# A Fourier-mixing and MLP kernel: one fold of the input rows is taken back, and the first transfers are put in another order

## The chip, the cores and the metric

The kernel runs on one core of a Trainium2 chip. The metric is the device time of one execution in microseconds. Three runs of the kernel before took 1938.29, 1939.47 and 1940.64 us; the median is 1939.47 us. A program that starts once does everything; the tables of sines and cosines are inputs, made ahead.

The engines are named as the profile names them: PE is TensorE (matmuls), PEld its weight loads, DVE is VectorE, ACT ScalarE, POOL GpSimd, and SP issues most of the transfers (SPq is its DMA queue).

## The reference

```python
batch, seq, dim = (8, 3008, 256)           # x: float32
n_tokens, d_model, d_ff = (24064, 256, 2048)   # w_in, w_out

def _attn_ref(x):
    X = np.fft.fft(x, axis=1)
    X = np.fft.fft(X, axis=2)
    return X.real.astype(np.float32)

def _moe_ref(x, w_in, w_out):
    h = x @ w_in
    r = np.maximum(h, 0.0)
    g = r * r
    return (g @ w_out).astype(np.float32)
```

The result of the first is reshaped to 24064 x 256 and goes into the second. Written out, the first is a transform of 3008 rows and one of 256 columns, of which the real part is kept. The weights come as 64-bit floats, which the kernel takes apart as words and turns into float32.

## The kernel before

With S = 3008 rows, the sums over n are folded by the symmetries of sine and cosine. The host sorts the rows so that n, S - n, S/2 - n and S/2 + n stand together for n from 0 to S/4. Sums and differences of these four, and of column pairs, leave 753 values of n. They are put into seven tiles of up to 128 rows in four classes: class 0, n = 0 mod 4 of the first half (1 tile), class 1, n = 2 mod 4 of the first half (1 tile), class 2, the odd n of the first half (tiles 2 and 3, 96 and 92 rows), class 3, the second half (tiles 4, 5 and 6). A class is multiplied with its own piece of the tables `cosT` and `sinT`, which lie in on-chip memory for the whole run. (The words that come with the change name the fold by "rows n of 2 mod 4"; in this code it is the tiles of class 2, `TWO` and `TWO + 1`.)

Class 3 is folded once more in batches 1 to 7 (n with its mirror), and in the kernel before class 2 is too: the second tile is loaded in reversed order, turned against the first, and two half-sized products take the place of a full one.

```python
    TWO = ODD0 - 2                 # ODD0 = 4, the first tile of class 3
    HALF2 = S // 32                # 94 rows
    ...
    def load_x(b, t):
        ...
        if b and t == TWO + 1:
            xt[b, t] = xp.tile([P, 4, D], F32, name="xt", tag="x")
            for p in range(0, ROWS2, R):
                at = TILES[TWO][1] + step * (2 * HALF2 - p - R)
                nc.sync.dma_start(out=xt[b, t][p:p + R], in_=x[b, at:at + step * (R - 1) + 1:step])
            return
    ...
    # in fold(b, t): the sums of the four rows (f_s, f_d, f_sc, f_dc, f_w), and for a folded tile
        def f_turn():
            w = w_of(t)
            if i != 1:
                st["v"], st["w"] = w_of(t - 1), w
                nc.vector.stream_shuffle(w[r], w[r], REVERSE)
            ...
            nc.scalar.copy(st["f0"][rows], st["v"][rows, 0])

        def f_even():
            v, w, a = st["v"][rows, 0], st["w"][rows, 0], st["f0"][rows]
            tt(out=v, in0=a, in1=w, op=ALU.add)
            tt(out=w, in0=a, in1=w, op=ALU.subtract)
        # f_sine: four products on ScalarE; f_odd: two scalar_tensor_tensor on VectorE
```

The products on TensorE, once for each batch, `which` (cosine or sine of the rows) and `kp` (even or odd k):

```python
            EVEN = ((0, 0, n2), (1, n2, n2), (2, 2 * n2, n1))     # n2 = 95 or 94, n1 = 189 or 188

            def even_n():
                st["ps"] = psd.tile([P, 512], F32, name="pd", tag="d")[0:n]
                for c, at, nk in EVEN:
                    if b and c == 2:
                        st["half"] = once_more(st["ps"][:, at:], c, nk)
                    else:
                        product(st["ps"][:, at:at + nk], c)       # L501: each tile of the class, nk columns
                copy_4()

            def once_more(ps, c, nk):                             # the products of L578
                nq = (nk + 2) // 2 if kp else (nk + 1) // 2
                pairs, rows = ((((TWO, TWO + 1),), HALF2), (((ODD0, ODD0 + 1), (ODD0 + 2, NT)), P))[c == 3]
                for part in range(2):
                    ...
                    for i, pair in enumerate(pairs):
                        nc.tensor.matmul(to, folded[b, pair[part != which]][0:rows, kp, PART[which]][:, 0:n],
                                         columns(tab, pairs[0][i] if c == 3 else TWO, o)[0:rows],
                                         start=i == 0, stop=i == len(pairs) - 1)
                if not kp:
                    return ps[:, 0:nk]
                a = hp.tile(...)                                  # for odd k: a copy on ScalarE,
                nc.scalar.copy(a, ps[:, 0:nq])                    # and join_odd: two operations on VectorE
                return a, ps[:, nq:2 * nq]
```

The steps that follow multiply with w_in (L664, L665, by way of the columns' transform G1 and G2), square on ScalarE, and multiply with w_out (L717, or L704 in the first steps). The folds and products of batch b + 1 are done in pieces between the steps of batch b, on VectorE, ScalarE and TensorE.

The first phase loads the first batch, both tables and the first weights on one queue, in this order, while VectorE folds:

```python
    for t in range(2):
        load_x(0, t)
    ...
    begin_win(0)                               # words of pair 0 of w_in: load, then convert
    ...
    load_table(cosT, cos_s, (2, 3))
    load_x(0, 6)
    load_table(cosT, cos_s, range(ODD0, NT))   # 3 transfers of 377 columns
    load_table(sinT, sin_s, range(ODD0, NT))   # 3 transfers of 377 columns
    win[1] = load(pair_in(1))                  # the second pair of w_in, 2 transfers
    load_table(sinT, sin_s, range(ODD0))       # 10 small transfers, of 95 or 189 columns
    win[2] = load(pair_in(2))                  # the third pair
    ...
    q_part("odd0", "odd1", "odd2")             # sine products on TensorE, tiles 4, 5, 6
    copy_e = win[0][2]()
    begin_win(1)                               # VectorE: L262, L267 and later L272 to L275
    for_q(3)
    q_part("even0", "even1", "even2")          # sine products, tiles 0 to 3
    awake(12)                                  # matmuls without use, to keep TensorE busy
    rounded(1)
    begin_win(2)                               # L262, L267 for the third pair
    for kp in range(2):
        for nm in ("join_4", "join_2", "lo"):
            groups[1, kp, nm]()                # VectorE: L538, L540
    spread_e()                                 # TensorE: L642, needs Qt
```

Each transfer of the queue waits, by a semaphore that the tile framework gives it in turn, until the transfer eight before it has landed.

Of the kernel before, what the change touches and what calls it, by code (L numbers as in the profile page):

```python
# [8 lines left out]
F32 = mybir.dt.float32  # L9
# [4 lines left out]
P = 128  # L14
R = 32
# [67 lines left out]
def kernel(  # L83
# [12 lines left out]
    nc = tc.nc  # L96
    B, NROW, _, D = x.shape
    S = out.shape[0] // B
# [35 lines left out]
    xt = {}  # L134
# [3 lines left out]
    ODD0 = NT - 3  # L138
# [4 lines left out]
           [(0, P, H // 2)] + [(H // 2 + p, 2 * HALF - P - p - R, R) for p in range(0, H // 2, R)]]  # L143
    assert H == P and REST <= H // 2 and TILES[ODD0][0] == 3 and TILES[ODD0 + 1][1] == TILES[ODD0][1] + P

    TWO = ODD0 - 2
    HALF2 = S // 32
    ROWS2 = TILES[TWO][3]
    assert TILES[TWO][0] == TILES[TWO + 1][0] == 2 and HALF2 <= ROWS2 < HALF2 + R and ROWS2 % R == 0

    def load_x(b, t):
        c, r0, step, rows = TILES[t]
        if b and c == 3:
            xt[b, t] = xp.tile([P, 4, D], F32, name="xt", tag="x")
            for p, first, count in ODD[t - ODD0]:
                nc.sync.dma_start(out=xt[b, t][p:p + count], in_=x[b, S // 8 + 1 + first:S // 8 + 1 + first + count])
            return
        if b and t == TWO + 1:
            xt[b, t] = xp.tile([P, 4, D], F32, name="xt", tag="x")
            for p in range(0, ROWS2, R):  # L160
                at = TILES[TWO][1] + step * (2 * HALF2 - p - R)
                nc.sync.dma_start(out=xt[b, t][p:p + R], in_=x[b, at:at + step * (R - 1) + 1:step])
            return

        while rows % 15 and rows % 16 and r0 + step * rows < NROW:
            rows += 1

        pool, tag = (gp, "g") if b == 0 and t < NT - NX else (xp, "x")
        xt[b, t] = pool.tile([P, 4, D], F32, name="xt", tag=tag)
        nc.sync.dma_start(out=xt[b, t][0:rows], in_=x[b, r0:r0 + step * (rows - 1) + 1:step])  # L170
# [151 lines left out]
    PQE = {}  # L322
    PART = (slice(0, H + 1), slice(H + 1, D))
    REVERSE = list(range(R - 1, -1, -1))

    turn = const.tile([P, 3, 3], F32, name="turn")

    def make_turn():
        for i, t in enumerate((ODD0, ODD0 + 1, TWO)):
            for a, tab in enumerate((cosT, sinT, sinT)):  # L330
                r = slice(0, TILES[t][3])
                nc.scalar.mul(turn[r, a, i:i + 1], tab[r, 1, PLACE[t]:PLACE[t] + 1], -1.0 if a == 2 else 1.0)
# [5 lines left out]
    def part_table(tab, t):  # L338


        nk, at = NC[0][TILES[t][0]], PLACE[t]
        rows = TILES[t][3]
        v = tab[0:rows, 0, at:at + nk]
        a = op.tile([P, nk], F32, name="tp", tag="os")[0:rows]
        nc.scalar.mul(a, v, rows_used if t == ODD0 + 1 else 1.0)
        nc.scalar.copy(v[:, 0:(nk + 1) // 2], a[:, 0::2])
        nc.scalar.copy(v[:, (nk + 1) // 2:], a[:, 1::2])

    def columns(tab, t, part):

        nk, at = NC[0][TILES[t][0]], PLACE[t]
        nq = (nk + 1) // 2
        return tab[:, 0, at + part * nq:at + (nk if part else nq)]

# [21 lines left out]
    def fold(b, t):  # L376


        odd, two = b > 0 and t >= ODD0, b > 0 and t == TWO + 1
        r = slice(0, P if odd else ROWS2 if two else TILES[t][3])  # L380
        st = {}

        def new(pool, nm, shape):
# [43 lines left out]
        if b == 0:  # L427
            return [f_s, f_d, f_sc, f_dc, lambda: (f_w(PART[0]), f_e()), lambda: f_w(PART[1])]
        ops = [(0.9, f_s), (0.9, f_d), (0.7, f_sc), (0.6, f_dc), (1.1, f_w)]
        if not (odd or two) or t == ODD0:  # L430
            return ops, None


        i = 2 if two else t - ODD0 - 1
        rows = slice(0, (P, REST, HALF2)[i])

        def f_turn():
            w = w_of(t)
            if i != 1:
                st["v"], st["w"] = w_of(t - 1), w  # L440
                nc.vector.stream_shuffle(w[r], w[r], REVERSE)
# [30 lines left out]
        return ops + [(0.8, f_turn), (1.3 if odd else 0.7, f_even), (0.2, f_sine)], (1.4 if odd else 1.2, f_odd)  # L472

    def dft_ops(b):

# [6 lines left out]
        def group(kp, which):  # L482
# [25 lines left out]
            def even_n():  # L508
                st["ps"] = psd.tile([P, 512], F32, name="pd", tag="d")[0:n]
                for c, at, nk in EVEN:  # L510
                    if b and c == 2:
                        st["half"] = once_more(st["ps"][:, at:], c, nk)
                    else:
                        product(st["ps"][:, at:at + nk], c)
                copy_4()

            def copy_4():
# [36 lines left out]
            def join_2():  # L554
                a, ps = st["b"], st["ps"]
                st["c"] = hp.tile([P, NC[0][3]], F32, name="dc2", tag="dc2", bufs=2)[0:n, 0:n0]
                both(st["c"][:, 0:n1], st["c"][:, n1:n0], a, st["half"] if b else ps[:, 2 * n2:2 * n2 + n1])

            def odd_part(i, lone_e):

# [5 lines left out]
            def once_more(ps, c, nk):  # L566

                nq = (nk + 2) // 2 if kp else (nk + 1) // 2
                pairs, rows = ((((TWO, TWO + 1),), HALF2), (((ODD0, ODD0 + 1), (ODD0 + 2, NT)), P))[c == 3]
                for part in range(2):  # L570
                    if kp:
                        tab, o = (cosT, sinT)[part], 0
                        to = ps[:, part * nq:part * nq + nq]
                    else:
                        tab, o = (cosT, sinT)[which], part
                        to = ps[:, part:nk:2]
                    for i, pair in enumerate(pairs):
                        nc.tensor.matmul(to, folded[b, pair[part != which]][0:rows, kp, PART[which]][:, 0:n],  # L578
                                         columns(tab, pairs[0][i] if c == 3 else TWO, o)[0:rows],
                                         start=i == 0, stop=i == len(pairs) - 1)  # L580
                if not kp:
                    return ps[:, 0:nk]
                a = hp.tile([P, NC[0][3] // 2 + 1], F32, name="oc", tag="oc", bufs=1)[0:n, 0:nq]
                nc.scalar.copy(a, ps[:, 0:nq])
                return a, ps[:, nq:2 * nq]

            def odd_n():
                ps = psd.tile([P, 512], F32, name="pd", tag="d")[0:n]
                st["odd"] = ps[:, 0:n0]
                if b is None:  # L590
                    return product(ps[:, 0:n0], 3)
                st["odd"] = once_more(ps, 3, n0)

            def join_odd(what, nk):

                a, ps = st[what]
                nq = a.shape[-1]
                st[what] = o = hp.tile([P, NC[1][3]], F32, name="do", tag="do", bufs=1)[0:n, 0:nk]
# [24 lines left out]
                return [((which, kp, nm), f) for nm, f in named]  # L623
            ops = [(0.1, even_n), (0.4, join_4), (0.5, join_2), (0.1, odd_n), (0.8, join_1)]
            if b and kp:
                ops.insert(4, (0.5, lambda: join_odd("odd", n0)))
                ops.insert(2, (0.4, lambda: join_odd("half", n1)))
            return ops

        ops = [] if b is None else [(0.0, start)]  # L630
# [158 lines left out]
    def ahead(b):  # L789
        start, *groups = dft_ops(b)  # L790
        if b == 1:

            tables = [(0.3, lambda tab=tab, t=t: part_table(tab, t)) for t in (TWO, ODD0, ODD0 + 1)
                      for tab in (cosT, sinT)]
            groups = [(1.5, fold_columns)] + dft_ops(None) + tables + groups
        groups.insert(0, start)

        pieces = []
        for ops, last in [fold(b, t) for t in range(NT)] + [(groups + [(0.0, lambda: load_e(b))], None)]:
            if held:  # L800
# [236 lines left out]
```

## Time and profile before

| what | us |
|---|---|
| median of three runs | 1939.47 |
| span of the profiled execution | 1936.3 |
| busy TensorE | 1924.3 (99%) |
| busy TensorE weight loads | 1711.0 (88%) |
| busy VectorE | 1424.3 (74%) |
| busy GpSimd | 1184.1 (61%) |
| busy ScalarE | 939.0 (48%) |

A busy share is an average over stages with different limits. A batch takes some 233 us (its products at L578 recur at that distance), and the first 110 us are a stage of their own, in which the tables and weights arrive and are converted. The timeline of an engine gives for each piece its start, its length, the line and the operation, output and input tiles with sizes, and how many instructions were merged; in brackets the idle time before it, and what ended it. Matmuls are pipelined, so that their lengths overlap; the distance from start to start is what one costs. A float32 matmul is recorded as two.

### The profile page before, as it was taken

What the parts mean: (1) busy time and instruction counts of PE and PEld (TensorE: products, weight loads), DVE (VectorE), ACT (ScalarE), POOL (GpSimd) and SP (SyncE); (2) the same over time, 40 slices, a digit from 0 to 9 for tenths busy, and PEclk for the clock granted to TensorE, in tenths of its full rate; (3) what the DMA queues carried; (4) which work ended last, traced back from release to release, by engine and by line L of the source; (5) the groups of instructions that cost most, each with busy time, mean ns of one, the idle gap of its engine ahead of it and who ended that gap; (6) DMA issues with size and microseconds to landing.
All of it is one profiled execution on the core that took longest, in us unless ns stands there. A gap on an engine that the chain in (4) does not pass through costs nothing.

```text
span 1936.3 us, 27908 instructions
## 1 busy us (share of the span) xinstructions
PE 1924.3 (99%) x9266; PEld 1711.0 (88%) x9266; DVE 1424.3 (74%) x3502; ACT 939.0 (48%) x1132; POOL 1184.1 (61%) x1708
## 2 busy tenths in 40 slices
PE   9999999999999999999999999999999999999998
PEld 7888888888988899888998889888898888988887
DVE  8999867777678776787667776777767777655554
ACT  2855554544445444445444454445534454444443
POOL 0047646676567665766667665667756776556655
PEclk9999999999999999999999999999999999999999
DMA  8341101111011101111011100111001100000000
GB/s 219 113 47 41 39 9 50 33 32 26 27 41 31 38 12 31 38 41 28 11 35 48 34 20 11 42 48 28 20 17 52 33 11 22 28 12 11 22 11 22
DMA packets 145788, 69.56 MB, mean 36 GB/s; under 512 B 129314, under 2 KB 136428, under 8 KB 145643
## 3 DMA queue, kind: packets, MB, share of 16 engines
q1 hardware_dynamic: 145184, 66.87, 13.4%
q8 instruction: 73, 1.20, 0.3%
q14 instruction: 72, 0.59, 0.1%
q0 software_dynamic: 176, 0.65, 0.1%
q10 hardware_dynamic: 283, 0.26, 0.0%
HBM read 43.03 MB, written 24.69 MB: 35 GB/s over the span
## 4 chain that ended last, share of the span: by engine, by line
PE 95%; DVE 4%; DMA 0%; issue 0%; ACT 0%; DVEq 0%; SPq 0%
PE ph L664 17%; PE ph L665 17%; PE mC L717 16%; PE mA L717 16%; PE mB L717 16%; PE mD L717 8%; PE pd L578 2%; PE pd L501 1%; DVE m L274 0%; DVE w L422 0%; DVE he L667 0%; DVE fd L272 0%; PE mA L704 0%; PE mB L704 0%; DVE g L670 0%
## 5 line engine op out<-in xcount | busy, mean ns | idle before, releaser
L679 ACT ACTIVATE g<-g 128x1004 f32<-128x1004 f32 (+1 forms) x384 | 399.4, 1040 | 783.6 <-DVE g L670 443.0
L667 DVE SCALAR_TENSOR_TENSOR he<-Et,gE,ph 128x251 f32<-128x251 f32 (+1 forms) x768 | 361.8, 471 | 385.7 <-PE ph L665 382.5
L687 POOL TENSOR_TENSOR s<-g 128x251 f32<-128x251 f32 (+1 forms) x376 | 248.5, 661 | 641.5 <-ACT g L680 510.2
L664 PE MATMUL ph<-Pt,G 128*128 128x251 f32 (+1 forms) x1536 | 452.5, 375 | 0.2 <-DVE g L670 0.2
L665 PE MATMUL ph<-Qt,G 127*128 127x251 f32 (+1 forms) x1536 | 452.2, 375 | 0.0
L680 ACT ACTIVATE g<-g 128x1004 f32<-128x1004 f32 (+1 forms) x384 | 399.3, 1040 | 12.2
L717 PE MATMUL mC<-s,wsum 128*128 128x251 f32 (+1 forms) x1504 | 381.4, 374 | 0.0
L717 PE MATMUL mA<-g,wout 128*128 128x251 f32 (+1 forms) x1504 | 379.9, 374 | 0.0
L669 DVE TENSOR_TENSOR g<-he,ph 128x251 f32<-128x251 f32 (+1 forms) x768 | 320.6, 418 | 54.5 <-DVE he L667 0.9
L665 PEld LDWEIGHTS ph<-Qt,G 127*128 127x128 f32 x1536 | 291.8, 190 | 35.9
L664 PEld LDWEIGHTS ph<-Pt,G 128*128 128x128 f32 x1536 | 287.0, 189 | 36.3 <-DVE dc L547 1.3
L717 PEld LDWEIGHTS mC<-s,wsum 128*128 128x128 f32 x1504 | 285.5, 190 | 34.5
L670 DVE TENSOR_TENSOR g<-he,ph 128x251 f32<-128x251 f32 (+1 forms) x768 | 314.5, 409 | 0.0
L717 PEld LDWEIGHTS mA<-g,wout 128*128 128x128 f32 x1504 | 282.6, 189 | 35.0 <-issue 0.3
L689 POOL TENSOR_TENSOR s<-g 128x251 f32<-128x251 f32 (+1 forms) x376 | 302.9, 806 | 0.0
L688 POOL TENSOR_TENSOR s<-s,g 128x251 f32<-128x251 f32 (+1 forms) x376 | 279.6, 744 | 29.5
L690 POOL TENSOR_TENSOR s<-g,s 128x251 f32<-128x251 f32 (+1 forms) x376 | 260.2, 692 | 0.0
L717 PE MATMUL mB<-g,wsum 128*128 128x251 f32 (+1 forms) x752 | 220.5, 374 | 0.0
L717 PE MATMUL mD<-s,wout 128*128 128x251 f32 (+1 forms) x752 | 220.3, 374 | 0.0
L717 PE MATMUL mB<-s,wout 128*128 128x251 f32 (+1 forms) x752 | 219.9, 374 | 0.0
L717 PEld LDWEIGHTS mB<-g,wsum 128*128 128x128 f32 x752 | 142.5, 190 | 17.5
L717 PEld LDWEIGHTS mD<-s,wout 128*128 128x128 f32 x752 | 141.9, 189 | 17.7
(139 smaller groups left out, 1355.5 us busy)
## 6 DMA issues: line engine op xcount, KB each, us to landing
out_dram<-os SPq DMA_DIRECT2D x376, 56.0 KB
xt<-in_x_dram SPq DMA_DIRECT2D x25, 384.0 KB
xt<-in_x_dram SPq DMA_DIRECT2D x63, 128.0 KB
Et<-e_dram SPq DMA_DIRECT2D x7, 752.5 KB
xt<-in_x_dram SPq DMA_DIRECT2D x9, 512.0 KB
out_dram<-os SPq DMA_DIRECT2D x288, 6.8 KB
raw<-in_moe_w_in_dram SPq DMA_DIRECT2D x16, 256.0 KB
raw<-in_moe_w_out_dram SPq DMA_DIRECT2D x16, 256.0 KB
```

Of the source, the lines that this page charges most:

```text
L664: nc.tensor.matmul(hP, G1[:, fs], pt[:, ks], start=True, stop=True)
L665: nc.tensor.matmul(hQ, G2[0:P - 1, fs], qt[0:P - 1, ks], start=True, stop=True)
L667: nc.vector.scalar_tensor_tensor(out=t, in0=et[:, ks], scalar=gE[:, fc:fc + 1], in1=hP, op0=ALU.mult, op1=ALU.add)
L669: tt(out=g[:, h, 0, 0:n], in0=t, in1=hQ, op=ALU.add)
L670: tt(out=g[:, h, 1, 0:n][:, ::-1], in0=t, in1=hQ, op=ALU.subtract)
L679: act(v, v, AF.Relu)
L680: act(v, v, AF.Square)
L687: gt(out=s1, in0=g21, in1=g22, op=ALU.add)
L688: gt(out=s2, in0=s1, in1=g11, op=ALU.subtract)
L689: gt(out=s3, in0=g11, in1=g21, op=ALU.subtract)
L690: gt(out=s4, in0=g12, in1=s2, op=ALU.subtract)
L717: nc.tensor.matmul(acc[nm][:, i, 0:n], w, v[:, 0:n], start=j == 0 and i == 0, stop=j == NJ - 1, skip_group_check=True)
```

## The change

It has two parts. The first takes back the additional fold of class 2: in batches 1 to 7 its two tiles are loaded, folded and multiplied as the rest is, with 189 or 188 columns for each. What is left of `once_more` serves class 3 alone. The second changes the first phase: the small transfers of the sine table stand in turns with its large ones (tile 4, tile 0, tile 5, tile 1, tile 6, tile 2), then the second pair of w_in, tile 3, and the third pair. It is for keeping enough bytes in flight, as only eight transfers may be.

```diff
-    TWO = ODD0 - 2
-    HALF2 = S // 32
-    ROWS2 = TILES[TWO][3]
...
     def load_x(b, t):
...
-        if b and t == TWO + 1:
-            xt[b, t] = xp.tile([P, 4, D], F32, name="xt", tag="x")
-            for p in range(0, ROWS2, R):
-                at = TILES[TWO][1] + step * (2 * HALF2 - p - R)
-                nc.sync.dma_start(out=xt[b, t][p:p + R], in_=x[b, at:at + step * (R - 1) + 1:step])
-            return
...
     def fold(b, t):
-        odd, two = b > 0 and t >= ODD0, b > 0 and t == TWO + 1
-        r = slice(0, P if odd else ROWS2 if two else TILES[t][3])
+        odd = b > 0 and t >= ODD0
+        r = slice(0, P if odd else TILES[t][3])
...
-        if not (odd or two) or t == ODD0:
+        if not odd or t == ODD0:
             return ops, None
...
             def even_n():
                 for c, at, nk in EVEN:
-                    if b and c == 2:
-                        st["half"] = once_more(st["ps"][:, at:], c, nk)
-                    else:
-                        product(st["ps"][:, at:at + nk], c)
+                    product(st["ps"][:, at:at + nk], c)
                 copy_4()
...
             if b and kp:
-                ops.insert(4, (0.5, lambda: join_odd("odd", n0)))
-                ops.insert(2, (0.4, lambda: join_odd("half", n1)))
+                ops.insert(4, (0.5, join_odd))
...
-            tables = [(0.3, lambda tab=tab, t=t: part_table(tab, t)) for t in (TWO, ODD0, ODD0 + 1)
-                      for tab in (cosT, sinT)]
+            tables = [(0.3, lambda tab=tab, i=i: part_table(tab, i)) for i in range(2) for tab in (cosT, sinT)]
...
     load_table(cosT, cos_s, range(ODD0, NT))
-    load_table(sinT, sin_s, range(ODD0, NT))
+
+    for t in range(ODD0, NT):
+        load_table(sinT, sin_s, (t, t - ODD0))
     win[1] = load(pair_in(1))
-    load_table(sinT, sin_s, range(ODD0))
+    load_table(sinT, sin_s, range(NT - ODD0, ODD0))
     win[2] = load(pair_in(2))
```

The parts that are left out fit the helper functions (the turning factors, the sorted table columns, `odd_n` and `join_odd`) to the one class that still uses them.

More of the change, by code (lines that the diff above doesn't have):

```diff
@@ L144 @@
     assert H == P and REST <= H // 2 and TILES[ODD0][0] == 3 and TILES[ODD0 + 1][1] == TILES[ODD0][1] + P
-    TWO = ODD0 - 2
-    HALF2 = S // 32
-    ROWS2 = TILES[TWO][3]
-    assert TILES[TWO][0] == TILES[TWO + 1][0] == 2 and HALF2 <= ROWS2 < HALF2 + R and ROWS2 % R == 0
     def load_x(b, t):
@@ L324 @@
     REVERSE = list(range(R - 1, -1, -1))
-    turn = const.tile([P, 3, 3], F32, name="turn")
+    turn = const.tile([P, 3, 2], F32, name="turn")
     def make_turn():
-        for i, t in enumerate((ODD0, ODD0 + 1, TWO)):
+        for i in range(2):
             for a, tab in enumerate((cosT, sinT, sinT)):
-                r = slice(0, TILES[t][3])
-                nc.scalar.mul(turn[r, a, i:i + 1], tab[r, 1, PLACE[t]:PLACE[t] + 1], -1.0 if a == 2 else 1.0)
+                nc.scalar.mul(turn[:, a, i:i + 1], tab[:, 1, PLACE[ODD0 + i]:PLACE[ODD0 + i] + 1], -1.0 if a == 2 else 1.0)
     rows_used = const.tile([P, 1], F32, name="rows_used")
@@ L336, with part_table @@
     nc.vector.memset(rows_used[0:REST], 1.0)
[L338 to L345, printed above, removed]
+    def part_table(tab, i):
+        nk, at = NC[0][3], PLACE[ODD0 + i]
+        v = tab[:, 0, at:at + nk]
+        a = op.tile([P, nk], F32, name="tp", tag="os")
+        nc.scalar.mul(a, v, rows_used if i else 1.0)
         nc.scalar.copy(v[:, 0:(nk + 1) // 2], a[:, 0::2])
@@ L349, in columns @@
     def columns(tab, t, part):
-        nk, at = NC[0][TILES[t][0]], PLACE[t]
+        nk, at = NC[0][3], PLACE[t]
         nq = (nk + 1) // 2
@@ L429, in fold @@
         ops = [(0.9, f_s), (0.9, f_d), (0.7, f_sc), (0.6, f_dc), (1.1, f_w)]
-        if not (odd or two) or t == ODD0:
+        if not odd or t == ODD0:
             return ops, None
-        i = 2 if two else t - ODD0 - 1
-        rows = slice(0, (P, REST, HALF2)[i])
+        i = t - ODD0 - 1
+        rows = slice(0, TILES[ODD0 + i][3] if i == 0 else REST)
         def f_turn():
             w = w_of(t)
-            if i != 1:
-                st["v"], st["w"] = w_of(t - 1), w
-                nc.vector.stream_shuffle(w[r], w[r], REVERSE)
+            if i == 0:
+                st["v"], st["w"] = w_of(ODD0), w
+                nc.vector.stream_shuffle(w, w, REVERSE)
             else:
@@ L470, in f_odd @@
                                                op0=ALU.mult, op1=ALU.add)
-        return ops + [(0.8, f_turn), (1.3 if odd else 0.7, f_even), (0.2, f_sine)], (1.4 if odd else 1.2, f_odd)
+        return ops + [(0.8, f_turn), (1.3, f_even), (0.2, f_sine)], (1.4, f_odd)
     def dft_ops(b):
@@ L556, in join_2 @@
                 st["c"] = hp.tile([P, NC[0][3]], F32, name="dc2", tag="dc2", bufs=2)[0:n, 0:n0]
-                both(st["c"][:, 0:n1], st["c"][:, n1:n0], a, st["half"] if b else ps[:, 2 * n2:2 * n2 + n1])
+                both(st["c"][:, 0:n1], st["c"][:, n1:n0], a, ps[:, 2 * n2:2 * n2 + n1])
             def odd_part(i, lone_e):
@@ L564, in odd_part @@
                 product(st["odd"], 3, lone_e, i)
[L566 to L585, printed above, removed]
             def odd_n():
@@ L591, in odd_n, with join_odd @@
                     return product(ps[:, 0:n0], 3)
-                st["odd"] = once_more(ps, 3, n0)
-            def join_odd(what, nk):
-                a, ps = st[what]
+                nq = (n0 + 2) // 2 if kp else (n0 + 1) // 2
+                for part in range(2):
+                    if kp:
+                        tab, o = (cosT, sinT)[part], 0
+                        to = ps[:, part * nq:part * nq + nq]
+                        other = part != which
+                    else:
+                        tab, o = (cosT, sinT)[which], part
+                        to = ps[:, part:n0:2]
+                        other = part != which
+                    for i, pair in enumerate(((ODD0, ODD0 + 1), (ODD0 + 2, NT))):
+                        nc.tensor.matmul(to, folded[b, pair[other]][:, kp, PART[which]][:, 0:n],
+                                         columns(tab, ODD0 + i, o), start=i == 0, stop=i == 1)
+                if kp:
+                    st["cos"] = hp.tile([P, nq], F32, name="oc", tag="oc", bufs=1)[0:n]
+                    nc.scalar.copy(st["cos"], ps[:, 0:nq])
+                    st["sin"] = ps[:, nq:2 * nq]
+            def join_odd():
+                a, ps = st["cos"], st["sin"]
                 nq = a.shape[-1]
-                st[what] = o = hp.tile([P, NC[1][3]], F32, name="do", tag="do", bufs=1)[0:n, 0:nk]
+                st["odd"] = o = hp.tile([P, NC[1][3]], F32, name="do", tag="do", bufs=1)[0:n, 0:n0]
                 tt(out=o[:, 0::2], in0=a[:, 0:nq - 1], in1=ps[:, 0:nq - 1], op=ALU.add)
```

## The prediction

> **What bounds the kernel now.** I read the shares of busy time first, then TensorE by stage.
>
> ```profile
> span 1936.3 us, 27908 instructions
> PE 1924.3 (99%) x9266; PEld 1711.0 (88%) x9266; DVE 1424.3 (74%) x3502; ACT 939.0 (48%) x1132; POOL 1184.1 (61%) x1708
> ...
> 0.00:110.00 110.00, 103.11 (x535) 88.58 (x536) 99.37 (x244) 60.88 (x108) 6.47 (x16) 0.98 0.55 153
> 110.00:285.00 175.00, 174.81 (x842) 151.62 (x841) 145.86 (x363) 88.78 (x121) 111.31 (x157) 1.00 0.18 33
> 285.00:1900.00 1615.00, 1615.00 (x7744) 1443.43 (x7743) 1163.06 (x2856) 776.06 (x891) 1048.58 (x1509) 1.00 0.11 28
> ```
>
> The last three lines give, for each stretch of the span, its length and the busy time of PE, PEld, DVE, ACT and POOL, then clock, DMA share and GB/s. From 110 to 1900 us TensorE lacks 0.19 us in all. So any TensorE time added there is added to the end, and work taken from DVE, ACT or POOL there buys nothing. Only the first 110 us (6.9 us idle) and the tail hold slack, and the change touches the first 45 us.
>
> Next, the batches. The products of the rows that are 2 mod 4 stand at L578 with 95 columns. In the timeline of TensorE each matmul is two records (x4 is two matmuls); the first column is the start, and starts are what count, as the records overlap.
>
> ```profile
> 269.06 0.80 PE L578 MATMUL pd<-cosT,w 128*128 128x189 f32 x4
> 269.70 0.80 PE L578 MATMUL pd<-sinT,w 128*128 128x189 f32 x4
> 270.34 0.59 PE L664 MATMUL ph<-Pt,G 128*128 128x250 f32 x2
> ...
> 271.19 0.58 PE L501 MATMUL pd<-sinT,w 95*127 95x95 f32 x4
> 271.61 0.61 PE L578 MATMUL pd<-sinT,w 94*127 94x95 f32 x4
> 272.05 1.04 PE L717 MATMUL mA<-g,wout 128*128 128x250 f32 x4
> ```
>
> Four records of 95 columns take 272.05 - 271.61 = 0.44 us, or 0.11 each; eight of 189 columns take 270.34 - 269.06 = 1.28 us, or 0.16 each. Half the columns thus cost 69% of the time.
>
> Last, the first phase: the timelines of VectorE and of the DMA queue, and DMA by stretch.
>
> ```profile
> 31.44 0.49 DVE L422 TENSOR_TENSOR w<-sc 120x127 f32<-120x127 f32 x2
> 32.00 0.43 DVE L262 TENSOR_SCALAR fd<-raw 128x512 uint32<-128x512 uint32 x1
> ...
> 35.57 0.69 DVE L275 SCALAR_TENSOR_TENSOR win<-m,fd 128x512 f32<-128x512 f32 x1
> 37.58 0.43 DVE L262 TENSOR_SCALAR fd<-raw 128x512 uint32<-128x512 uint32 x1 [1.32 <-DMA raw<-in_moe_w_in_dram]
> ```
>
> ```profile
> 20.37 1.51 SPq L247 DMA_DIRECT2D raw<-in_moe_w_in_dram  x2
> 22.49 10.96 SPq L194 DMA_DIRECT2D sinT<-in_sin_s_dram  x10
> 33.54 2.52 SPq L247 DMA_DIRECT2D raw<-in_moe_w_in_dram  x4
> ```
>
> ```profile
> 28.00:30.00 2.00, 2.00 (x8) 1.18 (x7) 1.97 (x6) 0.00 (x0) 0.00 (x0) 1.00 0.91 196
> 30.00:32.00 2.00, 2.00 (x8) 1.23 (x7) 1.86 (x5) 0.00 (x0) 0.00 (x0) 1.00 0.23 45
> 32.00:34.00 2.00, 2.00 (x8) 1.17 (x7) 1.93 (x5) 1.50 (x3) 0.00 (x0) 1.00 0.42 95
> 34.00:36.00 2.00, 2.00 (x14) 1.55 (x12) 1.97 (x5) 0.51 (x1) 0.00 (x0) 1.00 0.69 194
> ```
>
> VectorE carries the chain here: it starts the second pair of w_in at 32.00 without a wait, and stands 1.32 us at 37.58 for the third pair. That pair came late because ten small sine transfers in a row took the queue 10.96 us to issue (the instructions show why: each waits until the transfer eight before it has landed), and the DMA share fell to 0.23 meanwhile. TensorE then waits 1.6 us in front of L642 at 42.1 for Qt, the end of that VectorE chain.
>
> **What the Trainium skill says.** "TensorE: Matmul & The Clock Gate", section "LDWEIGHTS (loading the stationary operand)": a weight load costs by its columns, about P / 1.2 ns, and not by its rows; 128 columns give an estimate of 107 ns. The trace agrees: a 95-column pass with 94 weight rows and 128 weight columns starts every 111 ns, not in half the 160 ns of a 189-column one. So the short products of the kernel before are held by their weight loads. The same page, "What's actually happening": the clock gate falls to half after about 3.4 us of low activity. The trace shows one such fall, after the 2.25 us wait at 53.1: clock 0.50 from 54.0 to 57.4. "DMA: Bandwidth & Descriptors", section "Queues, rings and completion order": each ring takes its descriptors in order. The trace's completions agree: the transfers from 18 to 38 us land in the order of their issue.
>
> **The change, part by part.**
>
> (a) *The extra fold is removed.* In each of 7 batches there are 4 product groups (sums and differences of columns, k even and odd), 28 in all. Before: two matmuls on 94 rows with 95 columns, 4 records; over all 28 groups the distance to the next matmul is 442 to 448 ns, mean 445. After: two row tiles (of 96 and 92 rows) times 189 or 188 columns, 4 records of 0.160 us = 0.640. The first phase confirms this form: eight records at 96x189 run from 19.77 to 21.06 us, 0.161 each. Difference 0.195 us a group, times 28 = **+5.5 us** on a TensorE that does not pause there.
>
> (b) *VectorE and ScalarE are relieved.* Per batch DVE loses one shuffle (0.73), two sums (0.47 + 0.77), two turns (2 x 0.70) and four joins (4 x 0.25), 4.4 us; ACT loses a copy, four products and two copies, 0.39 + 4 x 0.39 + 2 x 0.24 = 2.4 us. Beside 230 us of a batch with TensorE full, this is worth **0**. The 0.19 us wait near 187 us may go.
>
> (c) *The first phase.* The new order of the queue is: sine tile 4, three small ones of tile 0, tile 5, three of tile 1, tile 6, two of tile 2, the second pair of w_in, two of tile 3, the third pair. The bytes are the same. What one transfer adds to the last landing while the engines are full, from the completions of the trace: a large sine one 1.3 to 1.8 us, a small one of 95 columns 0.16, one of 189 columns about 0.25, half a pair of w_in 0.6 to 0.7. Before, the three large ones had landed at 30.6 and the second pair at 31.9. After, there stand six at 0.16 and two at 0.25 ahead of that pair too, 1.5 us: it lands at about **33.4**, and VectorE, which takes its work in order, waits for it from 31.93, about 1.5 us, where it did not wait. For the third pair: two more small ones (0.5) and 1.3 give about **35.3**, instead of 37.5, as large transfers stay in flight and the hole of 30 to 36 us closes. From the first word of the second pair to the wait for the third VectorE has 4.2 us of work (32.00 to 36.2), so it arrives at 33.45 + 4.2 = 37.65, and the third pair is there. Against 37.58 that is +0.1 us. So one wait of 1.3 us is changed for another of about 1.5. My landing times are good to perhaps 0.7 us each way, and the change is meant to help; I put the first phase at **-0.2 us**, between -1.4 and +1.2.
>
> Sum: 1939.47 + 5.5 - 0.2 = **1944.8 us**.
>
> **Rivals.**
> 1. *The new order removes the wait and brings no new one.* Then VectorE gains all of 1.3 us, TensorE's 1.6 us at 42.1 nearly closes, and if the dense stretch then falls otherwise into the clock's window, the 3.4 us at half clock (1.7 us of TensorE time) may go as well. For it: DMA has a hole of about 3 us (0.77 + 0.58 + 0.31 of 2 us each). Against it: the second pair now stands behind 1.5 us of small transfers, and it was just in time before. It gives 5.5 - 1.3 = 1943.7, with the clock 1942.0.
> 2. *The small transfers break up the large ones.* Then sine tile 6 and the second pair land later still, at 34.5 or more, and VectorE loses over 1 us. For it: 380-byte rows move poorly (45 GB/s from 30 to 32 us). Against it: that low rate stands where the queue waited to issue, not where DMA was full. It gives about 1946.2.
> 3. *The fold's side work was costing more than it shows*, so that taking it off gives time back. Against it: TensorE has no idle time from 285 to 1900 us, and spacing of the main products (0.425 us a pair) is the same near the fold and away from it. It would give 1939 to 1941; I give it little.
> 4. *The longer products wait on something new*, such as the PSUM buffer that they fill. Against it: they use the same tile and number of matmuls. It would give 1948 or more.
>
> **Range and chances.** The 5.5 us is well founded, to 0.3. The first phase is uncertain by 1.2 us, the clock by up to 1.7, and three runs of the kernel before spread over 2.4 us. I take 1942.9 to 1946.9. A 2% move is 39 us, and nothing found here is a fifth of that: faster 0.01, same 0.98, slower 0.01.
>
> **What would show it.** Step (a): no 95-column products on 94 rows at the line of the extra fold, in their place four records at 189 columns that take 0.64 us from start to start in each of 28 groups, and busy TensorE up by about 5.5 us with still no idle time from 285 to 1900. Step (b): 63 DVE and about 57 ACT instructions fewer, span not shorter for it. Step (c): a DMA wait of 1 to 2 us ahead of the first L262 word operation near 32 us, none ahead of the one near 37.6, the queue's ten issues in a row gone, DMA share over 0.8 until about 34, and L642 on TensorE at 42.1 give or take 1 us. The prediction is wrong if idle time opens on TensorE in the batches, if the second pair lands by 32, or if the clock drops at another place or not at all.

## The result, and the profile after

The changed kernel takes 1946.18 us (median of 6 runs, 1944.48 to 1946.67) against 1938.53 us of the kernel before in its 6 runs: a ratio of 1.0037, 95% interval 1.0024 to 1.0049. It is slower by some 7 us, under 2%. The prediction was 1944.8 us, with 1942.9 to 1946.9.

First, TensorE by stretch in the changed kernel (length, then busy PE, PEld, DVE, ACT, POOL, clock, DMA share, GB/s):

```profile
span 1944.9 us, 27736 instructions
PE 1931.5 (99%) x9266; PEld 1717.6 (88%) x9266; DVE 1395.5 (72%) x3432; ACT 926.4 (48%) x1074; POOL 1175.6 (60%) x1708
...
0.00:110.00 110.00, 101.68 (x521) 87.26 (x522) 96.57 (x239) 58.72 (x101) 4.99 (x14) 0.97 0.53 153
110.00:285.00 175.00, 175.00 (x837) 151.78 (x836) 145.31 (x354) 86.82 (x110) 109.63 (x156) 1.00 0.20 31
285.00:1900.00 1615.00, 1615.00 (x7724) 1443.61 (x7723) 1131.78 (x2785) 763.23 (x846) 1036.91 (x1502) 1.00 0.14 29
```

TensorE is full from 110 to 1900 us, as before; only the first stretch has more idle time (8.3 us, before 6.9). VectorE lost 28.8 us and ScalarE 12.6 us of work, and nothing came of it.

Then the products, in the timeline of TensorE of the changed kernel. The eight records are four of 95 columns on classes 0 and 1, and now four of 189 columns on class 2:

```profile
273.85 0.59 PE L642 MATMUL ph<-Qt,G 127*128 127x250 f32 x2
274.28 1.25 PE L487 MATMUL pd<-sinT,w 95*127 95x95 f32 x8
275.36 1.01 PE L694 MATMUL mA<-g,wout 128*128 128x250 f32 x4
276.21 0.58 PE L694 MATMUL mB<-g,wsum 128*128 128x250 f32 x2
```

In the kernel before the same group started at 271.19 (shown in the prediction), and its mB here:

```profile
272.92 0.58 PE L717 MATMUL mB<-g,wsum 128*128 128x250 f32 x2
```

From the first record to the mB behind the group: 276.21 - 274.28 = 1.93 us, and before 272.92 - 271.19 = 1.73 us. The mA behind must be counted in, because the first long product behind a short one starts its successor 0.03 us late (0.19 in place of 0.16, or 0.24 in place of 0.21); in the kernel before that fell on mA, here it falls on the first 189-column one. Over all 28 groups the trace gives 36.87 us before and 42.42 after, each measured from the first record to the start of the second matmul behind the group: **+5.55 us**.

Last, the first phase: VectorE's timeline, and that of the DMA queue, in the changed kernel.

```profile
31.46 0.49 DVE L408 TENSOR_TENSOR w<-sc 120x127 f32<-120x127 f32 x2
35.05 0.43 DVE L251 TENSOR_SCALAR fd<-raw 128x512 uint32<-128x512 uint32 x1 [3.09 <-DMA raw<-in_moe_w_in_dram]
...
38.62 0.69 DVE L264 SCALAR_TENSOR_TENSOR win<-m,fd 128x512 f32<-128x512 f32 x1
39.23 0.42 DVE L251 TENSOR_SCALAR fd<-raw 128x512 uint32<-128x512 uint32 x1
```

```profile
18.94 10.90 SPq L183 DMA_DIRECT2D sinT<-in_sin_s_dram  x11
29.97 1.23 SPq L236 DMA_DIRECT2D raw<-in_moe_w_in_dram  x2
```

The wait for the third pair (1.32 us near 37.6) is gone, and one of 3.09 us for the second pair has come near 32. The second pair was issued at 30.0 and not at 20.4 us; by the last of its completions in the trace it landed at 34.95 and not at 31.91. The stretches of DMA show where the time went:

```profile
26.00:28.00 2.00, 1.83 (x6) 0.87 (x5) 1.93 (x6) 0.00 (x0) 0.00 (x0) 1.00 0.56 142
28.00:30.00 2.00, 2.00 (x7) 1.13 (x6) 1.97 (x7) 0.00 (x0) 0.00 (x0) 1.00 0.33 68
30.00:32.00 2.00, 2.00 (x8) 1.23 (x7) 1.89 (x5) 0.00 (x0) 0.00 (x0) 1.00 0.95 233
32.00:34.00 2.00, 2.00 (x8) 1.23 (x7) 0.00 (x0) 0.00 (x0) 0.00 (x0) 1.00 0.94 290
```

The hole in the DMA share that stood at 30 to 36 us did not close; it moved to 26 to 30 us. And one thing more, in the timeline of TensorE of the changed kernel:

```profile
43.76 1.04 PE L619 MATMUL pe<-Qt,ident 128*128 128x251 f32 x2 [2.59 <-DVE Qt L521]
44.59 1.04 PE L641 MATMUL ph<-Pt,G 128*128 128x251 f32 x2
45.42 1.04 PE L642 MATMUL ph<-Qt,G 127*128 127x251 f32 x2
```

These start 0.83 us apart where 0.42 is usual: behind the longer wait the clock stood at half from 44.0 to 47.4 us. The first phase adds up by the starts in both profiles, here before and then after:

```profile
42.11 0.69 PE L642 MATMUL pe<-Qt,ident 128*128 128x251 f32 x2 [1.64 <-DVE Qt L538]
43.74 0.48 DVE L667 SCALAR_TENSOR_TENSOR he<-Et,gE,ph 128x251 f32<-128x251 f32 x1 [0.59 <-PE ph L665]
94.20 0.69 PE L704 MATMUL mA<-g,wout 128*128 128x251 f32 x2 [0.58 <-DVE wout L275]
```

```profile
46.56 0.48 DVE L644 SCALAR_TENSOR_TENSOR he<-Et,gE,ph 128x251 f32<-128x251 f32 x1 [1.76 <-PE ph L642]
97.14 0.69 PE L681 MATMUL mA<-g,wout 128*128 128x251 f32 x2 [0.58 <-DVE wout L264]
```

L642 of before (L619 after) comes 1.65 us later (43.76 - 42.11), VectorE's first step behind it 2.82 us later (46.56 - 43.74), and the last product with w_out that waits, the end of this phase, 2.94 us later (97.14 - 94.20). With 5.55 us of the groups that is 8.5, and the two spans are 8.6 us apart.

### The profile page after: what moved, and what is told of

The parts are those of the page before. It is cut to its first block, busy times and chain, and to the rows that moved or that the text cites. A ratio compares the mean times of both kernels' runs of the same rounds, so it can differ in the third digit from the quotient of the medians.

```text
span 1944.9 us, 27736 instructions
## 1 busy us (share of the span) xinstructions
PE 1931.5 (99%) x9266; PEld 1717.6 (88%) x9266; DVE 1395.5 (72%) x3432; ACT 926.4 (48%) x1074; POOL 1175.6 (60%) x1708
## 4 chain that ended last, share of the span: by engine, by line
PE 95%; DVE 3%; DMA 1%; SPq 0%; issue 0%; ACT 0%; DVEq 0%
PE ph L641 17%; PE ph L642 17%; PE mC L694 16%; PE mA L694 16%; PE mB L694 16%; PE mD L694 8%; PE pd L487 2%; PE pd L565 2%; DMA xt<-in_x_dram 1%; DMA sinT<-in_sin_s_dram 0%; DVE m L263 0%; DVE fd L261 0%; DVE he L644 0%; PE mA L681 0%; PE mB L681 0%
## 5 line engine op out<-in xcount | busy, mean ns | idle before, releaser
L642 PE MATMUL ph<-Qt,G 127*128 127x251 f32 (+1 forms) x1536 | 452.3, 375 | 0.0
L642 PEld LDWEIGHTS ph<-Qt,G 127*128 127x128 f32 x1536 | 292.0, 190 | 36.2
L641 PEld LDWEIGHTS ph<-Pt,G 128*128 128x128 f32 x1536 | 288.1, 189 | 35.4 <-DVE g L647 0.7
L665 POOL TENSOR_TENSOR s<-s,g 128x251 f32<-128x251 f32 (+1 forms) x376 | 275.0, 731 | 29.5
L667 POOL TENSOR_TENSOR s<-g,s 128x251 f32<-128x251 f32 (+1 forms) x376 | 254.2, 676 | 0.0
```

What stands on the lines that cost most here:

```text
L641: nc.tensor.matmul(hP, G1[:, fs], pt[:, ks], start=True, stop=True)
L642: nc.tensor.matmul(hQ, G2[0:P - 1, fs], qt[0:P - 1, ks], start=True, stop=True)
L665: gt(out=s2, in0=s1, in1=g11, op=ALU.subtract)
L667: gt(out=s4, in0=g12, in1=s2, op=ALU.subtract)
```

## The experiments

Each run was timed beside the kernel before on the same chip, so that a ratio is to be compared with another ratio, more than a time with a time. Theory: the two parts add up, 28 longer product groups on a full TensorE and a first phase that waits for the second pair. Rivals: the products cost all of it; or small transfers slow the large ones; or the side work that was taken off has an effect of its own.

**The new order alone.** The kernel before with the four lines of the order:

```diff
-    load_table(sinT, sin_s, range(ODD0, NT))
+    for t in range(ODD0, NT):
+        load_table(sinT, sin_s, (t, t - ODD0))
     win[1] = load(pair_in(1))
-    load_table(sinT, sin_s, range(ODD0))
+    load_table(sinT, sin_s, range(NT - ODD0, ODD0))
```

> The kernel before with the new order of the sine table alone; the extra fold stays. Theory: the second pair of w_in lands late, near 34.9 us as in the changed kernel (31.9 before), VectorE waits some 3 us for it near 32 us and no longer 1.3 us for the third pair, and the first phase ends later: +2 to +3 us, 1940.5 to 1941.5. Rival, the whole change of +7.6 us comes from the products and the clock happened to fall otherwise: within 0.5 us of the kernel before, 1938.0 to 1939.0.

Measured: 1940.86 us against 1938.95, ratio 1.0008 (1.0000 to 1.0016). The second pair landed at 34.05 us, VectorE waited 2.02 us for it and none for the third, and L642 came at 42.85. The rival that puts everything on the products falls by the profile; by the times alone the interval just reaches 1. The clock fell to half here too, from 44.3 to 47.7 us, and the last product with w_out that waits came at 95.92, 1.7 us later than before.

**The fold taken back alone.** The changed kernel with the old order (the diff above, reversed).

> The changed kernel with the old order of the sine table; the extra fold is gone. Theory: 28 product groups at 0.640 in place of 0.445 us on a full TensorE, +5.5 us, so 1943.5 to 1944.5, and the first phase as in the kernel before. Rival, the products cost all of the change: +7.6 us, 1946. If the parts do not add up, this run and that with the new order alone differ from the whole by more than 1 us.

Measured: 1944.24 us against 1938.95, ratio 1.0026 (1.0015 to 1.0037), +5.3 us; the 28 groups take 42.42 us, as in the changed kernel. The two parts together, 0.0008 + 0.0026 = 0.0034, agree with the whole, 0.0037, within the intervals. In this run's profile the second pair landed at 32.77 us, VectorE waited 0.63 us for it, and L619 came at 42.91, 0.8 us later than L642 in the kernel before, although the order is the same. A difference of under 1 us between single profiles of the first phase therefore says little.

**The second pair ahead of tile 6.** On the kernel before:

```diff
-    load_table(sinT, sin_s, range(ODD0, NT))
+    load_table(sinT, sin_s, (ODD0, 0, ODD0 + 1, 1))
     win[1] = load(pair_in(1))
-    load_table(sinT, sin_s, range(ODD0))
+    load_table(sinT, sin_s, (ODD0 + 2, 2, 3))
     win[2] = load(pair_in(2))
```

> The kernel before with the sine table's transfers in turns (tile 4, 0, 5, 1, then the second pair of w_in, then 6, 2, 3 and the third pair). Theory (it is the place of the second pair that costs, not the turns): the pair lands by 32 us, VectorE does not wait there, the third pair lands near 36, and the time is 0.5 to 1.3 us under the kernel before, 1937.2 to 1938.0. Rival (small transfers between large ones slow the large ones): the second pair lands after 33 us nonetheless and the time is 1 us or more over the kernel before.

Measured: 1937.56 us against 1938.95, ratio 0.9993 (0.9985 to 1.0001). The second pair landed at 30.51 us, the third at 35.64, and VectorE waited for neither. The first line is a stretch of the DMA share, the others are VectorE's timeline:

```profile
26.00:28.00 2.00, 1.99 (x7) 1.24 (x8) 1.90 (x6) 0.00 (x0) 0.00 (x0) 1.00 0.17 45
```

```profile
31.29 0.49 DVE L422 TENSOR_TENSOR w<-sc 120x127 f32<-120x127 f32 x2
31.70 0.42 DVE L262 TENSOR_SCALAR fd<-raw 128x512 uint32<-128x512 uint32 x1
...
35.87 0.42 DVE L262 TENSOR_SCALAR fd<-raw 128x512 uint32<-128x512 uint32 x1
36.21 0.42 DVE L267 TENSOR_SCALAR m<-raw 128x512 uint32<-128x512 uint32 x1
37.40 0.32 DVE L538 SCALAR_TENSOR_TENSOR db<-pd,signs,da 128x95 f32<-128x95 f32 x1 [0.77 <-ACT da L519]
```

Turns of small and large transfers make a hole here too (a DMA share of 0.17 from 26 to 28 us), but nothing that is waited for stands behind it; what costs is the place of the second pair. A wait of 0.77 us for the copy of the even sine products has come in the place of the 1.32.

**Tile 6 ahead of the small ones of tile 1.** On the kernel before, with the order 4, 0, 5, 6, 1, 2, second pair, 3, third pair:

```diff
-    load_table(sinT, sin_s, range(ODD0, NT))
+    load_table(sinT, sin_s, (ODD0, 0, ODD0 + 1, ODD0 + 2, 1, 2))
     win[1] = load(pair_in(1))
-    load_table(sinT, sin_s, range(ODD0))
+    load_table(sinT, sin_s, (3,))
     win[2] = load(pair_in(2))
```

> The kernel before with the new order of the sine table, but tile 6 ahead of the small transfers of tile 1 (4, 0, 5, 6, 1, 2, second pair, 3, third pair). Theory (in the new order three times two large transfers have six small ones between them, and tile 6 waits, as the ninth, until tile 4 has landed at 27.5 us: the hole in the DMA share moved to 26 to 30 us in place of closing): tile 6 is issued near 22.5 us and not 27.5, no stretch of 2 us from 26 to 34 us has a DMA share under 0.7, and the second pair lands 1 to 2 us earlier than in the run with the new order alone (34.0), so 32.0 to 33.0; the time is 1 us or more under that run's ratio of 1.0008, at or under the kernel before. Rival (the second pair is late by the bytes ahead of it alone): it lands after 33.5 and the time is that of the new order alone.

Measured: ratio 0.9999 (0.9990 to 1.0007), 1938.42 us against 1939.08. Tile 6 was issued at 22.2 us (27.3 in the run with the new order alone), and the hole is gone:

```profile
26.00:28.00 2.00, 2.00 (x7) 1.15 (x7) 1.90 (x6) 0.00 (x0) 0.00 (x0) 1.00 1.03 238
28.00:30.00 2.00, 2.00 (x8) 1.20 (x7) 2.00 (x6) 0.00 (x0) 0.00 (x0) 1.00 0.79 163
30.00:32.00 2.00, 2.00 (x8) 1.23 (x7) 1.72 (x5) 0.00 (x0) 0.00 (x0) 1.00 0.94 285
```

The second pair landed at 32.37 us with the same bytes ahead of it as in the run with the new order alone, 1.7 us earlier than there, and VectorE waited 0.68 us. Some 0.6 us of the 1.7 is that the whole queue ran earlier in this profile (tile 4 landed at 26.70 and not at 27.32). From the landing of tile 4 to that of the second pair it takes 4.3 to 4.8 us in the four profiles with the old order, 6.7 to 7.4 us in the five with the new order, and 5.7 us here. So, as far as one profile tells, about half of the lateness came from the bytes ahead of the pair and half from the hole. That the total is less than with the new order alone is likely, but the two intervals overlap.

**One to one.** On the kernel before, after tiles 4 and 5 one small transfer each, one after each half of the second pair, then tile 6, two small ones, and two after each half of the third pair:

```diff
-    load_table(sinT, sin_s, range(ODD0, NT))
-    win[1] = load(pair_in(1))
-    load_table(sinT, sin_s, range(ODD0))
-    win[2] = load(pair_in(2))
...
+    for t in (ODD0, ODD0 + 1):
+        load_table(sinT, sin_s, (t,))
+        some()                            # one of the ten small ones
+    win[1] = load(pair_in(1), some)       # and one after each half
+    load_table(sinT, sin_s, (ODD0 + 2,))
+    some(2)
+    win[2] = load(pair_in(2), lambda: some(2))
```

> The kernel before with large and small transfers one to one: 4, small, 5, small, second pair with a small one after each half, 6, two small, third pair with two small ones after each half. Theory: about half of the eight transfers in flight are large at any time, the DMA share stays over 0.7 from 26 to 34 us, the second pair lands by 31 us, VectorE waits for no pair, and the time is that of the run with the second pair ahead (ratio 0.9993), since TensorE's even products set the pace there. Rival (turns of small and large cost bandwidth): the pairs land later than in that run and the time is at or over the kernel before.

Measured: 1937.75 us against 1939.08, ratio 0.9994 (0.9986 to 1.0002). The DMA share is 0.78 to 1.04 in every 2 us from 26 to 36, the second pair landed at 30.81 us, and VectorE waits for no pair; its only wait from 32 to 43 us is 0.95 us for the copy of the even products. The time cannot be told from that with the pair ahead: once no pair is waited for, a fuller DMA brought nothing that shows.

**The even products earlier.** The run with the second pair ahead, L299 behind the even sine products, and two useless matmuls fewer:

```diff
-    copy_e = win[0][2]()
     begin_win(1)
     for_q(3)
     q_part("even0", "even1", "even2")
-    awake(12)
+    copy_e = win[0][2]()
+    awake(10)
```

> The run with the second pair ahead of tile 6, and the product of L299 moved behind the even sine products, for which VectorE waited 0.8 us there. Theory: the even products end 0.4 us earlier and VectorE's joins with them: 0.3 to 0.5 us under the run with the pair ahead, ratio 0.9990 to 0.9992, some 1.5 to 1.9 us under the kernel before. Rival (another wait takes its place at once): the same ratio as that run, 0.9993.

Measured: 1938.09 us against 1939.08, ratio 0.9996 (0.9987 to 1.0004). VectorE's wait for the copy fell from 0.77 to 0.17 us, and the end did not follow: the products with w_out wait for VectorE's conversions, 1.5 us in four waits against 1.3 in three, and the last of these products came at 93.17 us against 93.28. The profile speaks for the rival; the interval of the times takes in both.

**The side work left out.** In the kernel before the turning of class 2 (one shuffle, two sums and two turns on VectorE, five operations on ScalarE in each batch) is left out; loads, half-sized products and joins stay. What it computes lacks that step.

```diff
-        if not (odd or two) or t == ODD0:
+        if not odd or t == ODD0:
             return ops, None
```

> The kernel before with the extra fold's turning left out for class 2 (in each of 7 batches one shuffle, two sums and two turns on VectorE, five operations on ScalarE), with its loads, its half-sized products and their joins kept. This leaves a part of the computation out. Theory: VectorE loses some 3.3 us a batch and nothing comes of it, since TensorE is full: within 0.5 us of the kernel before. Rival (the side work costs TensorE time): 1 us or more under the kernel before.

Measured: 1944.97 us against 1938.95, ratio 1.0033 (1.0020 to 1.0046): less work, and 6 us more. Neither the theory nor the rival had this. The page's waits of TensorE have a new first line, and its timeline one long gap:

```profile
PE pd L501 <- DVE we L372: 3.5, 1, 3.5
...
228.61 0.59 PE L665 MATMUL ph<-Qt,G 127*128 127x251 f32 x2
232.72 1.97 PE L501 MATMUL pd<-cosT,we 95*7 95x95 f32 x8 [3.52 <-DVE we L372]
```

The kernel shares its side work out between the steps by weights. With some of it gone the rest moved, and once, in batch 0, the products of the column sums were in TensorE's order ahead of the sums, which stood behind ScalarE's squares and four turns. Behind the gap the clock was at half from 232.9 to 236.3 us, some 1.7 us of TensorE's time. From 285 us on TensorE was full again.

**The side work empty, but in its place.** The same, with pieces of the same weights that do nothing:

```diff
+    def nothing():
+        pass
...
+        if two:
+            return ops + [(0.8, nothing), (0.7, nothing), (0.2, nothing)], (1.2, nothing)
```

> The kernel before with the extra fold's turning of class 2 left out (part of the computation is missing), but with empty pieces of the same weights in its place, so that all other side work stays where it was between the steps. Theory: the 6 us that the first such run lost came from side work that moved to another place in batch 0, and the relief itself is worth nothing: within 0.7 us of the kernel before, no wait for the column sums near 229 us. Rival 1 (the relief itself slows the kernel): again +5 us. Rival 2 (side work costs TensorE time): 1 us or more under the kernel before.

Measured: 1938.94 us against 1939.67, ratio 0.9995 (0.9987 to 1.0004), and no gap:

```profile
110.00:285.00 175.00, 175.00 (x843) 152.19 (x842) 144.03 (x358) 87.80 (x117) 110.34 (x157) 1.00 0.18 33
285.00:1900.00 1615.00, 1615.00 (x7744) 1445.42 (x7743) 1145.13 (x2821) 767.05 (x861) 1042.66 (x1509) 1.00 0.11 28
```

The relief itself is worth nothing that can be told from zero; the 6 us came from the move. The changed kernel moved its side work as well, and there no gap arose.

**Fewer columns.** In the changed kernel the second product of class 2 takes 95, then 48, of its columns in batches 1 to 7. Both leave part of the sums out.

```diff
+                    nk = 95 if b and c == 2 and t == ts[-1] else NC[kp][c]     # and 48
...
-                                     (cosT if lone_e else tab)[0:rows, kp, PLACE[t]:PLACE[t] + NC[kp][c]],
+                                     (cosT if lone_e else tab)[0:rows, kp, PLACE[t]:PLACE[t] + nk],
...
```

> The changed kernel, in batches 1 to 7 the second of the two class 2 products takes the first 95 columns alone; this leaves out part of the sums. Theory (short products are held by their weight loads, 0.11 us a record): the four records of a group take 2 x 0.16 + 2 x 0.11 = 0.54 us in place of 0.64, 28 groups save 2.8 us, about 1943.4. Rival (a product costs by its columns): 2 x 0.16 + 2 x 0.08 = 0.48, 4.5 us less, about 1941.7.

> As the kernel with 95 columns, but with 48; this leaves out more of the sums. Theory: no less time than with 95, as the weight load of 128 columns stays: 0.54 us a group, about 1943.4. Rival: 2 x 0.16 + 2 x 0.04 = 0.40 us a group, 6.7 us less than the changed kernel, about 1939.5.

Measured: ratios 1.0019 (1.0011 to 1.0027) and 1.0018 (1.0010 to 1.0027), 1943.50 and 1943.21 us against 1939.67. The timeline of TensorE with 95 columns, then with 48:

```profile
273.50 1.12 PE L488 MATMUL pd<-sinT,w 95*127 95x95 f32 x8
274.46 1.04 PE L695 MATMUL mA<-g,wout 128*128 128x250 f32 x4
275.33 0.58 PE L695 MATMUL mB<-g,wsum 128*128 128x250 f32 x2
```

```profile
272.13 1.08 PE L488 MATMUL pd<-sinT,w 95*127 95x95 f32 x8
273.05 1.08 PE L695 MATMUL mA<-g,wout 128*128 128x250 f32 x4
273.96 0.58 PE L695 MATMUL mB<-g,wsum 128*128 128x250 f32 x2
```

275.33 - 273.50 and 273.96 - 272.13 are both 1.83 us, 0.10 under the changed kernel; over the 28 groups it is 39.63 us in each, 2.79 less than 42.42. Taking off half of the columns once more saves nothing at all: what the shorter product saves, the mA behind it loses. The rival, a cost by columns alone, falls; by the times too, since with 48 columns it would be near the kernel before, a ratio of about 1.0002.

That the floor belongs to the weight load, and not to a record as such, the trace of the kernel before shows. Near 231 us its column sums multiply the same columns of the table with 7 weight columns in place of 127 or 128:

```profile
231.21 0.41 PE L501 MATMUL pd<-cosT,we 95*7 95x95 f32 x3
231.46 0.48 PE L501 MATMUL pd<-cosT,we 96*7 96x189 f32 x2
```

The second to fourth record take 231.46 - 231.21 = 0.25 us, 0.083 each. With 127 weight columns the same three, from 271.27 to 271.61 us, take 0.11 each.

**More useless matmuls.** The changed kernel, to keep TensorE busy while it waits for Qt:

```diff
-    awake(12)
+    awake(22)
```

> The changed kernel with 22 in place of 12 of the useless matmuls ahead of L642, so that they fill about 2.4 of the 2.6 us in which TensorE waits for Qt. Theory (part of the loss in the first phase is the clock's fall to half near 44 us, which delays the products that VectorE waits for by 1.2 us): the clock stays full there and the time is about 1 us under the changed kernel, 1945.0 to 1945.5. Rival (the clock's fall costs nothing as VectorE sets the pace): within 0.4 us of the changed kernel, 1945.8 to 1946.6.

Measured: 1945.33 us against 1939.67, ratio 1.0030 (1.0019 to 1.0040). In its profile the wait of 2.59 us is 0.18, and the clock does not fall there:

```profile
44.15 0.69 PE L619 MATMUL pe<-Qt,ident 128*128 128x251 f32 x2 [0.18 <-DVE Qt L521]
44.68 0.59 PE L641 MATMUL ph<-Pt,G 128*128 128x251 f32 x2
45.10 0.59 PE L642 MATMUL ph<-Qt,G 127*128 127x251 f32 x2
```

From L619 to VectorE's first step behind it are 1.63 us, in the changed kernel 2.80, so 1.2 us of that kernel's first phase are the clock in these profiles. The other profiles agree. Take the first product that waits for Qt and the last product with w_out that waits, and compare both with the kernel before. In the eight runs with such a last wait and no fall of the clock near 44 us, the two have moved by the same, to 0.1 us. In the three with that fall (the changed kernel, the new order alone, 95 columns) the last one has moved 1.0 to 1.3 us more. The fall does not always come: with 48 columns, in the same order, the clock stayed full behind a wait of 2.44 us. By the times this run and the changed kernel cannot be told apart, as the intervals of 1.0030 and 1.0037 overlap.

## Why the prediction was right, and where not

(a) *The products, +5.5 us: right.* They cost 5.55 us over the 28 groups, and 5.3 us alone in time. The reason given, a floor of 0.11 us from the weight load of 128 columns, held against its rival with 95 and 48 columns, and records with 7 weight columns do not have it. One detail was missed: a long record behind a short one takes 0.03 us more, on whichever side of the group it stands; it cancels in the sum.

(b) *The relief, 0: right*, by the run with empty pieces. That the pieces also set where everything else stands was not seen, and could have cost 6 us.

(c) *The first phase, -0.2 us: wrong.* Alone it cost 0.0008 of the time (0 to 0.0016), 1.6 us; in the profiles it is 1.7 us alone and 2.9 us in the changed kernel. The exchange of one wait for another was right in kind: the third pair is no longer waited for, and the second is. The step that failed reads "large transfers stay in flight and the hole of 30 to 36 us closes". A transfer waits for the eighth ahead of it, and of the eight ahead of tile 6 in the new order six are small: tile 6 waited for tile 4, and the hole moved to 26 to 30 us. The second pair landed at 34.1 to 35.4 us in five profiles where 33.4 was worked out, VectorE waited 2.0 us for it alone and 3.1 in the changed kernel where 1.5 was set down, and it came to the third pair at 39.23 where 37.65 was worked out. The term for the bytes was sound: 33.4 is 5.8 us behind the landing of tile 4, and with tile 6 ahead, which closed the hole, it was 5.7. The second term missing was the clock's fall near 44 us, 1.2 us in the profile, which had been named as a risk but not put to the wait that the change lengthens. By the prediction's own signs this part was wrong: the clock dropped at another place, the DMA share was 0.33 and not over 0.8 from 28 to 30 us, and L642 came 1.65 us later where 1 us was allowed.

Of the rivals, the second (small transfers break up the large ones) came nearest, with tile 6 and the second pair later, over 1 us lost, and 1946.2 us. Its reason, that rows of 380 bytes move poorly, is not what held tile 6 up: issued ahead of the small transfers of tile 1, it left no hole. The first fell by the wait of 3.09 us, the third by the run with empty pieces, and the fourth as TensorE has no idle time from 110 to 1900 us.

The total fell in the range since (a) is three times (c), and with some luck: the prediction started from 1939.47 us, and the median of six runs of the kernel before is 1938.53. Of the change itself, 5.3 us were predicted and 7.65 measured.

Three orders are at or under the kernel before (0.9993, 0.9994, 0.9996), each with an interval that just takes in 1. That the second pair ahead of tile 6, with the extra fold kept, beats both kernels is shown against the changed one and only likely against the kernel before.

## What to carry to other kernels

Where the number of transfers in flight is limited, count the bytes among them and not the transfers, and put first what the engine that sets the pace asks for first: a hole in the DMA share did no harm here unless something that is waited for stood behind it. A matmul with few columns costs its weight load (0.11 us a record with 128 weight columns here), so going from 189 to 95 columns saved a third and not a half, and from 95 to 48 nothing. And where side work is shared out by weights, taking a piece out moves all the others; put an empty one in its place before believing what its removal cost.

## What had not been expected of the hardware

The distance to the next matmul depends on the one ahead of it: a 48-column record starts its own successor after 46 ns, the next one then after 110, and the 250-column one behind after 280 ns in place of 213. The weight load that was not hidden is paid one or two records later, so a group must be measured to the second instruction behind it. The clock fell to half for 3.4 us behind waits of 1.90 us (95 columns), 1.99 (new order alone), 2.25 (the kernel before), 2.59 (the changed kernel) and 3.52 (side work left out), and for 6.8 us at one of 2.25 (tile 6 ahead). It did not fall behind one of 2.25 with the second pair ahead, nor behind one of 2.44 with 48 columns. So the length of the wait alone does not decide it, and most of these waits are shorter than the 3.4 us of low activity that the prediction took for it; what decides was not tried.
